# A spectrum in one matmul stage: five row blocks of weighted sines in place of sixteen blocks and a butterfly

## The chip, the cores and the metric

The kernel runs on one core of one Trainium2 chip. The metric is the device time of one execution in microseconds (us). Engines: PE (TensorE; its weight loads are counted apart, as PEld), DVE (VectorE), ACT (ScalarE), POOL (GpSimd) and SP (SyncE, which here only issues DMA transfers). Each engine works through its own instructions in their order; it waits for others by semaphores.

## The reference, cut to what matters

Two independent parts are computed, and their outputs stand side by side. Part A is a recurrent attention over 64 segments of 32 rows, which the change does not touch. Part B is a state-space layer: for each of 1024 channels d, a kernel of 2048 values is made from 128 complex exponentials, and the input u is convolved with it by transforms of twice the length.

```python
P = jnp.exp(logdA[:, :, None] * l[None, None, :])
K = jnp.einsum('dn,dnl,dn->dl', Cc, P, dB).real
Kf = jnp.fft.rfft2(Kp...)            # K, padded to 4096
Uf = jnp.fft.rfft2(up...)            # u, padded to 4096
y = jnp.fft.irfft2(Uf * Kf, ...)[..., :L] + u * Dskip
```

## The kernel before, in words

Part B runs first (0 to 670 us), part A after it (to the end at 2019.6 us). All of part B is in `part_b`; its order is written out by hand.

*Few different values.* The kernel's values are worked out at 641 of the 2048 places only: every place up to 256, every second one to 512, every fourth to 1024, every eighth to 2048 (row 640 is the last). In between, the nearest lower or upper one stands. These 641 rows are `Kd` in device memory.

*Parameters and matrices* (up to about 100 us). Sines and cosines of 16 row blocks by 4 frequency groups are made into `MF`. The transform of 4096 values is split by residue r of the place modulo 4, so that `MF` serves the kernel, the input u and (transposed, as `MI`) the way back.

*Table rounds* (about 100 to 390 us). The loop `for f in range(-1, 17)` (L1191) runs through the words of `ORDER` (L661); a word with a prime belongs to the round before. Round f makes the values of 64 channels: PE makes exponents and phases (`X..p`, `X..t`), ACT takes eight exponentials E (L1139), loads another table, and takes sine and cosine (`S`, `C`); DVE makes `wn` (L1165, word `w`), the absolute value (`b`), and the products gi and gr (L1113, L1114); PE sums the products (`K`), DVE copies the sums (`x`) into a tile `KxT`, one for each half of the channels, two buffers. The words P, U and M in between are side work: projections of part A (`P`), spectra of the input u (`U`, for the 16 blocks below, to `Ud` in device memory) and transposes of `MF` (`M`, L940, copied at L944 and written to `MId` by POOL at L945). When a half is complete, `put_values` writes its rows from `KxT` to `Kd` in 44 pieces (L1020). Those of the first half go out one at each exponential of the rounds after; those of the second half ("late writes") after round 16, from the queues of SP (24) and POOL (20) in turn.

*Loading the kernel's values.* `load_k` (L1024) fetches them back, repeated as the 2048 places need them: 32 to 64 small transfers into 16 blocks of 128 rows, `KT`. `negate` makes a negated copy of 8 of the blocks.

*Blocks.* Then come 16 blocks b: four quarters of 256 channels (dq) by four frequency groups (kc). For each,
- `spectrum` (L1091): 64 matmuls of 128x128 by 128x256 (L1101) into two PSUM tiles `hps`, one for the even and one for the odd residues;
- `odd` (L1259, three copies on ACT) and `pointwise` (L1264, DVE): sum and difference of the two tiles (`X`, L1265 and 1266), which are two frequencies n_ = 0, 1 apart by half the range; four multiplications with the spectrum of u (`us`, loaded by `load_u`), two sums, and two more to `Bt`;
- from b = 4 on, two `inverse` (L1324 and on) of an earlier quarter: 32 matmuls back each (`products_back`), a copy by ACT (L1339), a multiplication and a sum by DVE (L1342, 1343), and a transfer out.

Spectrum b+1 stands ahead of pointwise b and of the two inverses in PE's order. Blocks 0 to 3 have no inverses. Pool `ps_h` has 2 buffers up to block 3 and 3 buffers of one tile after, `ps_y` has 2. After block 15 eight inverses are left. The SBUF tiles x, y and osb of `pointwise` are in the pool `b_pw`, which takes space that the pools of the table rounds (`b_tab`, `b_kx` with `KxT`, `b_tmp`) gave back; a tile that overlaps one of them waits for whoever still reads it.

*Weights of part A.* `residents` loads 39 tiles of part A's weights into space that part B gives back; a dictionary in the block loop says how many at each block.

Of the kernel before, what the change touches and what calls it, by code (L numbers as in the profile page):

```python
# [662 lines left out]
def part_b(ctx, tc, u, A_re, A_im, B_re, B_im, C_re, C_im, log_dt, Dskip, out_b, ahead, copies, residents, first_state):  # L663
# [32 lines left out]

    par_t = [tabs.tile([128, 8, 128], BF16, name="pt%d" % n_) for n_ in range(2)]
# [337 lines left out]

    def load_k(d0, n_d, qs, KT, later=None):
        dsl = slice(d0, d0 + n_d)

        def rows(r0, n, step=1):
            return Kd[r0:r0 + step * (n - 1) + 1:step, dsl]  # L1040
        n_q = [0]

        def get(out, in_):
            q = qs[n_q[0] % len(qs)]
            n_q[0] += 1
            if later is None:
                q.dma_start(out=out, in_=in_)
            else:
                later.append(lambda: q.dma_start(out=out, in_=in_))
        for r in (0, 2, 1, 3):  # L1050
            k0 = KT[:, 4 * r, :]
            get(k0[0:64], rows(r, 64, 4))
            get(k0[64:128], rows(256 + (0, 0, 1, 2)[r], 64, 2))
            k1 = KT[:, 4 * r + 1, :]
            if r == 2:
                get(k1[0:128:2], rows(384, 64, 2))
                get(k1[1:128:2], rows(386, 64, 2))
            else:
                get(k1[:], rows(384 + (0, 0, 0, 1)[r], 128))
            for mc in (2, 3):  # L1060
                k2 = KT[:, 4 * r + mc, :]
                q0 = 512 + 64 * (mc - 2)
                get(k2[0:128:2], rows(q0, 64))
                if r == 0:
                    get(k2[1:128:4], rows(q0, 32, 2))
                    get(k2[3:128:4], rows(q0 + 2, 32, 2))
                else:
                    get(k2[1:128:2], rows(q0 + 1, 64))
        return KT
# [9 lines left out]
    KNs = []  # L1079

    def negate(KT, eng=None):
        KN = ahead.pool.tile([128, 8, DH], BF16, name="KN", tag="xTl")
        if eng:
            eng.tensor_scalar(out=KN[:], in0=KT[:, 8:16, :], scalar1=-1.0, scalar2=None, op0=ALU.mult)
        else:
            for i in range(2):
                sc.activation(out=KN[:, :, DQ * i:DQ * i + DQ], in_=KT[i][:, 8:16, :], func=ACT.Copy, scale=-1.0)
        KNs.append(KN)

    def spectrum(b, s_):  # L1090
        dq, kc = b // 4, b % 4  # L1091
        KN = KNs[dq // 2]
        d = slice(DQ * (dq % 2), DQ * (dq % 2) + DQ)
        KT = ks[0][:, :, d] if dq < 2 else ks[dq - 1][:]
        for half in range(2):
            for r in range(2):
                for cs in range(2):
                    for i, rr in enumerate((r, r + 2)):
                        for mc in range(4):
                            rhs = KN[:, 4 * (rr - 2) + mc, d] if half == 1 and i == 1 else KT[:, 4 * rr + mc, :]  # L1100
                            pe.matmul(s_[r][half][:, cs, :], lhsT=MF[:, kc, 4 * rr + mc, cs, :], rhs=rhs,  # L1101
                                      start=(i == 0 and mc == 0), stop=(i == 1 and mc == 3), skip_group_check=True)
# [94 lines left out]
    for eng, names in ((sc.copy, ON_ACT), (v.tensor_copy, ON_DVE)):  # L1197
        for nm, kind, slot in names:
            evict_of[nm] = (kind, slot, eng)
    for f in range(-1, 17):  # L1200
        if f == 15:
            for kind, slot in sorted(k for k in pending if k[0] == "P"):
                run_evict(kind, slot, v.tensor_copy)
            while ahead.late:
                ahead.late.pop(0)()
            ks = [load_k(0, DH, (sy, gp), ahead.pool.tile([128, 16, DH], BF16, name="KT", tag="kst"))]
        if f == 16:
            spectra = [load_u(0), load_u(1)]
        for word in ORDER:
            nm, r = word.rstrip("'"), f - word.endswith("'")  # L1210
            if f == 16 and word == ORDER[0]:
                s0 = ps_e.tile([128, 2, 512], F32, name="pa", tag="pa")
                s1 = [ps_t.tile([128, 512], F32, name="ptt", tag="ptt") for _ in range(2)]
                first = [[s0[:, half, :].rearrange("p (c d) -> p c d", c=2) for half in range(2)],
                         [t_[:].rearrange("p (c d) -> p c d", c=2) for t_ in s1]]
                negate(ks[0], v)
                spectrum(0, first)
            if nm in evict_of:
                run_evict(*evict_of[nm])
            elif nm[0] in side_ops:  # L1220
                if f >= 0 and r >= 0:
                    run_side(nm[0], int(nm[1:] or 0))
            elif nm[0] == "X":
                e = int(nm[1])
                if 0 <= r <= 15 - (e == 0) or (r == -1 and e == 0):
                    table_ops[nm[2]](r, e)
            elif 0 <= r <= 15:
                table_ops[nm[:-1]](r, int(nm[-1]))
    for n_, f_ in enumerate(late):
        f_((sy, gp)[n_ % 2])  # L1230
# [20 lines left out]
    KT2 = [pool.tile([128, 16, DQ], BF16, name="KT", tag="KT%d" % i) for i in range(2)]  # L1251
    MI = [pool.tile([128, 2, 2, 4, 128], BF16, name="MI", tag="MI%d" % i) for i in range(8)]
    resident = residents(pool, [MF[:, kc].rearrange("p c a n -> p (c a n)")[:, 2048 * i:2048 * i + 2048] for kc in range(4) for i in range(2)])

    def odd(s_):
        o_ = pw.tile([128, 2, 2, DQ], F32, name="osb_", tag="o")
        sc.copy(out=o_[:, 0], in_=s_[1][0])
        sc.activation(out=o_[:, 1, 0], in_=s_[1][1][:, 1, :], func=ACT.Copy, scale=-1.0)
        sc.copy(out=o_[:, 1, 1], in_=s_[1][1][:, 0, :])  # L1259
        return o_  # L1260

    def pointwise(b, s_, o_):
        kc, Bt, us = b % 4, Bs[b // 4], spectra.pop(0)
        X = pw.tile([128, 2, 2, 2, DQ], F32, name="x", tag="x")  # L1264
        v.tensor_tensor(out=X[:, 0], in0=s_, in1=o_[:], op=ALU.add)  # L1265
        v.tensor_tensor(out=X[:, 1], in0=s_, in1=o_[:], op=ALU.subtract)  # L1266
        Y = pw.tile([128, 2, 2, 2, DQ], F32, name="y", tag="y")
        for n_ in range(2):
            uc, un = (us[n_][:, :, i, :].unsqueeze(2).to_broadcast([128, 2, 2, DQ]) for i in range(2))
            v.tensor_tensor(out=Y[:, n_], in0=uc, in1=X[:, n_], op=ALU.mult)  # L1270
            v.tensor_tensor(out=X[:, n_], in0=un, in1=X[:, n_], op=ALU.mult)
        Yc, Xc = (t_[:].rearrange("p a b c d -> p (a b) c d") for t_ in (Y, X))
        v.tensor_tensor(out=Yc[:, :, 0, :], in0=Yc[:, :, 0, :], in1=Xc[:, :, 1, :], op=ALU.subtract)
        v.tensor_tensor(out=Yc[:, :, 1, :], in0=Yc[:, :, 1, :], in1=Xc[:, :, 0, :], op=ALU.add)
        for j, op in ((0, ALU.add), (1, ALU.subtract)):
            v.tensor_tensor(out=Bt[:, kc, j], in0=Y[:, 0], in1=Y[:, 1], op=op)

# [36 lines left out]
    def products_back(yp, dq, c, neg, mn, kcs):  # L1314
        r, Bt = c // 4, Bs[dq]
        j = r % 2
        for b in range(2):
            for kc in kcs:
                for cs in range(2):
# [26 lines left out]
    keys = []  # L1346
# [3 lines left out]
    ctx_h = ExitStack()  # L1350
    ps_h = ctx_h.enter_context(tc.tile_pool(name="b_psh0", bufs=2, space=PSUM))

    def halves(t_):
        return [t_[:, half] for half in range(2)]
    now = s0[:].rearrange("p h (c d) -> p h c d", c=2), odd(first)
    for b in range(16):
        dq = b // 4
        if b % 4 == 0:
            Bs[dq] = (bp0, bp)[dq % 2].tile([128, 4, 2, 2, 2, DQ], BF16, name="Bt", tag="B")
        if b == 0:  # L1360
            ks += [load_k(DQ * i, DQ, (sy, gp), KT2[i - 2], keys) for i in (2, 3)]
        if b == 3:
            nxt = [load_inverse(*todo[n_]) for n_ in range(NIV)]
            pointwise(b, *now)
            ctx_h.close()
            ctx_p.close()
            ps_h = ctx.enter_context(tc.tile_pool(name="b_psh", bufs=3, space=PSUM))
            ps_y = ctx.enter_context(tc.tile_pool(name="b_psy", bufs=2, space=PSUM))
        if b + 1 < 16:
            s_ = [ps_h.tile([128, 2, 2, DQ], F32, name="hps", tag="h") for _ in range(2)]  # L1370
            spectrum(b + 1, [halves(t_) for t_ in s_])
            then = s_[0][:], odd([halves(t_) for t_ in s_])
        if b != 3:
            pointwise(b, *now)
        now = then
        if b + 2 < 16:
            spectra.append(load_u(b + 2))
        for _ in range(min(16, len(keys)) if b >= 2 else 0):
            keys.pop(0)()
# [3 lines left out]
        for _ in range({1: 1, 2: 1, 3: 1, 6: 4, 11: 2, 12: 2, 13: 4, 14: 4}.get(b, 0)):  # L1383
# [8 lines left out]
        if b == 6:  # L1392
            negate(ks[1:])
# [4 lines left out]
    for n_ in range(8):  # L1398
        inverses(1)
        for _ in range((11, 5)[n_] if n_ < 2 else 1):  # L1400
            next(resident, None)
    while unsent:
        unsent.pop(0)()

# [27 lines left out]
def kernel(  # L1432
# [34 lines left out]
    def residents(stay, early):  # L1467
# [5 lines left out]
        four = ahead.pool.tile([128, 4, 2048], BF16, name="W4", tag="kst")  # L1473
        for t_ in [four[:, i, :] for i in range(4)]:
            put(t_)
            yield
        for n in range(2):
            for t_ in early[0:6] if n == 0 else early[6:8]:
                put(t_)
                yield  # L1480
            two = stay.tile([128, 2, 2048], BF16, name="W2", tag="KT%d" % n)
            for i in range(2):
                put(two[:, i, :])
                yield
# [77 lines left out]
```

## Time and profile before

| what | value |
|---|---|
| three runs, us | 2025.39, 2012.65, 2023.66 (median 2023.66) |
| profiled execution: time, span, us | 2021.33, 2019.6 |
| mean granted TensorE clock | 0.986 |
| busy over the span: PE, DVE, ACT, POOL | 91%, 71%, 47%, 22% |
| part B ends, last product back (L1324) | 669.7 us |
| rounds f = 0 to 15: one from the next | 20.05 us |
| block 0's first DVE sum | 429.87 us |
| block 4's first product back | 484.8 us |
| from one block to the next, 4 to 14 | 14.0 us |

The profile is of one execution; times inside it count from its start. The views quoted below have these forms. By stage: start:end, length, then the busy time of PE, PEld, DVE, ACT and POOL with the number of instructions, the granted clock (1.00 is full), DMA share and GB/s. Timelines: start, length, engine, line of the kernel, operation, output<-input, shape, and in brackets the idle time before it and who ended it; instructions of one kind that follow each other closely are one row (x64). An engine's name with q is its DMA queue.

### The profile page before, as it was taken

Reading aid. Unit: us, or ns where it says so; the run is one execution under the profiler, and the core shown is the slowest. Engines: PE = TensorE matmul, PEld = TensorE weight load, DVE = VectorE, ACT = ScalarE, POOL = GpSimd, SP = SyncE. Lnnn points to the kernel's source line nnn. Section 1 sums busy time; section 2 is a strip of 40 time slices with the busy share of each in tenths; the row PEclk is TensorE's granted clock in tenths of the full one; section 3 lists DMA queues with packets and bytes.
Section 4 is the critical chain, followed back from the end, with each engine's and each line's share of the span. In section 5 each row is a group of like instructions: output and inputs, shape, how many; then the busy total and the mean of one; then the engine's idle time right before and its main releaser. Section 6 shows DMA issues by size and latency. Waiting matters only on the chain.

```text
span 2019.6 us, 75101 instructions
## 1 busy us (share of the span) xinstructions
PE 1835.2 (91%) x32170; PEld 1154.4 (57%) x32198; DVE 1437.1 (71%) x3442; ACT 949.2 (47%) x1662; POOL 440.1 (22%) x864
## 2 busy tenths in 40 slices
PE   1699999778999789999999999999999999999998
PEld 1365766567888445555555555555555555555554
DVE  8879999999998356766667666666766666676650
ACT  4888898831333334344444434344444434344430
POOL 2135555547000011111111111111111111111120
PEclk9999999998999889999999999999999999999999
DMA  6788996868456999999999999999999999999991
GB/s 172 187 231 270 265 269 179 221 188 264 153 158 231 343 326 348 339 336 345 345 345 350 332 335 353 344 335 344 351 324 343 346 344 352 336 349 332 345 346 40
DMA packets 352630, 591.60 MB, mean 293 GB/s; under 512 B 111312, under 2 KB 229408, under 8 KB 350248
## 3 DMA queue, kind: packets, MB, share of 16 engines
q1 hardware_dynamic: 297452, 527.25, 77.2%
q10 hardware_dynamic: 44812, 28.26, 4.6%
q0 software_dynamic: 10032, 31.28, 4.4%
q8 instruction: 252, 4.13, 0.8%
q14 instruction: 82, 0.67, 0.1%
HBM read 531.12 MB, written 66.05 MB: 296 GB/s over the span
## 4 chain that ended last, share of the span: by engine, by line
PE 37%; DMA 23%; DVE 4%; issue 1%; ACT 1%; POOL 0%; SPq 0%; ACTq 0%; DVEq 0%; POOLq 0%
PE acc L375 21%; DMA wst<-WD_v 9%; PE pp L488 8%; DMA wst<-WD_o 7%; PE pe L625 3%; DMA wst<-WD_k 2%; PE tr L386 2%; DMA wst<-WD_q 2%; DMA arena<-PKd 2%; PE pv L460 1%; PE pv L456 1%; DVE arena L582 1%; PE sc L400 1%; DVE arena L441 1%; ACT arena L582 1%
## 5 line engine op out<-in xcount | busy, mean ns | idle before, releaser
L375 PEld LDWEIGHTS <-a_hT 128*32 128x32 bf16 x12352 | 326.4, 96 | 320.0 <-issue 60.9
L381 ACT CAST arena<-acc 128x512 bf16<-128x512 f32 x384 | 224.7, 585 | 396.2 <-PE acc L375 320.8
L375 PE MATMUL acc<-W,a_hT 128*32 128x512 bf16 x4608 | 354.1, 381 | 0.0
L488 PEld LDWEIGHTS <-arena 128*32 128x32 bf16 x8256 | 217.2, 97 | 86.8 <-issue 63.4
L375 PE MATMUL acc<-wst,a_hT 128*32 128x512 bf16 x2304 | 229.6, 382 | 29.3 <-DMA wst<-WD_v 22.0
L389 POOL COPY arena<-arena 128x128 bf16<-128x128 bf16 x128 | 37.4, 292 | 840.7 <-DMA arena<-PKd 315.6
L296 DVE TENSOR_SCALAR arena<-keep 128x256 int32<-128x256 int32 (+1 forms) x512 | 175.4, 394 | 29.5 <-PE acc L375 28.3
L375 PE MATMUL acc<-MF,a_hT 128*32 128x512 bf16 x2048 | 172.0, 382 | 0.0
L488 PE MATMUL pp<-W_o,arena 128*32 128x256 bf16 x4096 | 138.2, 275 | 5.0 <-DMA W_o<-in_A_Wo_dram 5.0
L168 PE MATMUL pro<-xTl,wsl 128*128 128x512 bf16 x490 | 113.0, 383 | 12.5 <-ACT xTl L112 6.6
L415 DVE TENSOR_REDUCE a_mx<-sc 128x4 f32<-128x160 f32 (+1 forms) x192 | 71.6, 373 | 73.6 <-PE sc L403 71.8
L419 ACT ACTIVATE sc<-sc 128x160 f32<-128x160 f32 (+1 forms) x192 | 63.9, 333 | 122.6 <-DVE sc L416 121.9
L1101 PEld LDWEIGHTS <-MF 128*128 128x128 bf16 x1024 | 102.5, 100 | 30.8 <-issue 8.2
L503 DVE COPY arena<-tr 128x512 bf16<-128x512 bf16 x64 | 27.2, 425 | 126.7 <-PE tr L386 126.7
L423 DVE TENSOR_REDUCE a_mx<-sc 128x4 f32<-128x160 f32 (+1 forms) x192 | 72.8, 379 | 55.3 <-ACT sc L419 54.9
L1101 PE MATMUL hps<-KT,MF 128*128 128x256 bf16 x720 | 94.2, 283 | 15.0 <-DVE x L1266 11.1
L1139 ACT ACTIVATE E<-pa 128x648 bf16<-128x648 f32 x128 | 90.9, 710 | 33.1 <-PE pa L1131 27.9
L1324 PE MATMUL yp<-Bt,MI 128*128 128x256 bf16 x680 | 102.8, 273 | 0.7 <-ACT yb L1339 0.7
L450 POOL TENSOR_TENSOR arena<-arena,a_BD 128x128 bf16<-128x128 bf16 x128 | 51.1, 399 | 234.0 <-DVE arena L433 221.5
L582 ACT CAST arena<-pp 128x128 bf16<-128x128 f32 x64 | 17.0, 265 | 163.2 <-DVE arena L582 163.2
L168 PEld LDWEIGHTS <-wsl 128*128 128x128 bf16 x512 | 50.5, 99 | 72.0 <-issue 16.2
L375 PE MATMUL acc<-W_v,a_hT 128*32 128x512 bf16 x1280 | 91.1, 378 | 0.0
(330 smaller groups left out, 3892.1 us busy)
## 6 DMA issues: line engine op xcount, KB each, us to landing
wst<-WD_v SPq DMA_DIRECT2D x256, 512.0 KB
wst<-WD_k SPq DMA_DIRECT2D x192, 512.0 KB
wst<-WD_o SPq DMA_DIRECT2D x192, 512.0 KB
wst<-WD_q SPq DMA_DIRECT2D x128, 512.0 KB
Ud<-ux POOLq DMA_DIRECT2D x16, 1024.0 KB, 5.9
uq<-Ud SPq DMA_DIRECT2D x32, 512.0 KB
wsl<-in_A_Wk_dram SPq DMA_DIRECT2D x16, 512.0 KB
wsl<-in_A_Wv_dram SPq DMA_DIRECT2D x16, 512.0 KB
```

What stands on the lines that cost most here:

```text
L168: nc.tensor.matmul(a[:], lhsT=w[:, kc, 128 * j:128 * j + 128], rhs=xTl[:, kc, :, :].rearrange("p s k -> p (s k)"), start=(kc == 0), stop=( ...
L296: nc.vector.tensor_scalar(out=out.bitcast(I32), in0=in_.bitcast(I32), scalar1=0, scalar2=None, op0=ALU.bitwise_or)
L375: nc.tensor.matmul(a[32 * g:32 * g + 32, o_:o_ + rhs.shape[1]], lhsT=hT[:, kc, :], rhs=rhs, start=(kc == 0), stop=(kc == KC - 1), tile_pos ...
L381: nc.scalar.copy(out=q, in_=a[:])
L415: nc.vector.tensor_reduce(out=m_, in_=x, axis=AX.X, op=ALU.max)
L419: nc.scalar.activation(out=flat(sc, i), in_=flat(sc, i), func=ACT.Exp, scale=scale)
L423: nc.vector.tensor_reduce(out=m_, in_=x, axis=AX.X, op=ALU.add)
L488: nc.tensor.matmul(po[32 * qt:32 * qt + 32, o_:o_ + rhs.shape[1]], lhsT=oT[:, h % 4, (h % 16) // 4, :], rhs=rhs, start=False, stop=(h == 3 ...
L625: nc.tensor.matmul(pe[n][:], lhsT=left[2 * b + hi // 16][:, 128 * (hi % 16):128 * (hi % 16) + 128], rhs=wo[u][:, 1024 * hh + 512 * n:1024 ...
L1101: pe.matmul(s_[r][half][:, cs, :], lhsT=MF[:, kc, 4 * rr + mc, cs, :], rhs=rhs, start=(i == 0 and mc == 0), stop=(i == 1 and mc == 3), ski ...
L1139: sc.activation(out=T["E", r, e // 4][:, lo:lo + 8 * NE].rearrange("p (i c) -> p i c", i=2), in_=T.pop(("p", r, e))[:, :, 0:4 * NE], func= ...
L1324: pe.matmul(yp[:, b, :], lhsT=m_[:, b, cs, kc, :], rhs=Bt[:, kc, j, half, c_, :], start=(kc == 0 and cs == 0 and half == 0), stop=(kc == 3 ...
```

## The change

The spectrum is made from the 640 different values themselves, in five blocks of 128 rows: row 0 to 255 in two, then one for each coarser range. A value that stands for several places is one sine times a weight that depends on the frequency alone; the places of a coarse row are put at the middle of its range, and the weights make up for it.
- **Matrices G.** For each group kc, n_, row block j, cosine or sine and half there is a 128x128 matrix. `columns_of_turns` makes the rows' and frequencies' digits (22 small operations on DVE, 25 on POOL) when round f = 3 begins, ahead of all of its words; `turned_columns` transposes them in the P slots of round 15. `build` then multiplies them (matmuls of 7 rows into a PSUM bank: angles in turns), and ACT takes the sine of each bank (`sine_of`, 11 of 512 columns for a group; 3 more copies for the weights). `weighted` multiplies three of the row blocks by their weights on DVE, twice a group.
- **Spectrum.** 40 matmuls for a block: five row blocks, for each n_, half, and cosine or sine. Each n_ has its own PSUM tile; nothing is summed or negated afterwards. `odd`, `negate` and the two sums `X` go. The multiplications read PSUM. All of Kd's 640 rows of a half come by one transfer.
- **Row 640** enters on the way back: one matmul of four rows for every second inverse (`l4`, `w4`, made from `Kd[640]` and rows of u by POOL).
- **Order.** At f = 16 a list of its own, `LAST`, is run, with the matrices of group 0 and the spectrum of block 0; U2 and U3 move from round 16 to 15; the last transposes' copy (`M0`) goes from DVE to ACT. The load of u for block 1 stands behind the second `weighted` of group 0. Groups 1 to 3 are built during blocks 0 to 2.
- **Weights of part A.** 39 loads as before, into other tiles; by block 14, 19 as before, at other blocks.

The core of the diff:

```diff
+    g_l = tabs.tile([128, 14, 7], BF16, name="g_l")
+    g_r = tabs.tile([128, 4, 4, 7], BF16, name="g_r")
...
+    def load_k(half, KT):
+        sy.dma_start(out=KT, in_=Kd[0:640, DH * half:DH * half + DH].rearrange("(j p) d -> p j d", p=128))
+        return KT
+
+    def columns_of_turns():
+        at = tabs.tile([128, 6], I32, name="g_at")
+        for j, (b0, step) in enumerate(((0, 2), (256, 2), (512, 4), (1024, 8), (2048, 16), (0, 2))):
+            gp.iota(at[:, j:j + 1], pattern=[[1, 1]], base=b0, channel_multiplier=step)
+        atF = tabs.tile([128, 6], F32, name="g_atF")
+        v.tensor_copy(out=atF[:], in_=at[:])
...
+    def sine_of(out, bank):
+        sc.activation(out=out, in_=bank.bitcast(I16)[:, 0:1024:2], func=ACT.Sin, scale=float(TWO_PI / 65536))
...
+    def weighted(kc, n_, amp):
+        a_ = amp.rearrange("p (j q) -> p j q", j=3)[:, :, 256 * n_:256 * n_ + 256]
+        g_ = G[kc][:, n_, 2:5].rearrange("p j s h f -> p j s (h f)")
+        v.tensor_tensor(out=g_, in0=g_, in1=a_.unsqueeze(2).to_broadcast([128, 3, 2, 256]), op=ALU.mult)
...
-    def spectrum(b, s_):
...
-                    for i, rr in enumerate((r, r + 2)):
-                        for mc in range(4):
-                            rhs = KN[:, 4 * (rr - 2) + mc, d] if half == 1 and i == 1 else KT[:, 4 * rr + mc, :]
-                            pe.matmul(s_[r][half][:, cs, :], lhsT=MF[:, kc, 4 * rr + mc, cs, :], rhs=rhs,
+    def spectrum(b, n_, outs):
...
+            for cs in range(2):
+                for j in range(5):
+                    pe.matmul(outs[half][:, cs, :], lhsT=G[kc][:, n_, j, cs, half, :], rhs=KT[:, j, d], ...)
...
+    LAST = ("w0' b0' C0' b1' gi0' C1' G0 gr0' w1' gr1' gi1' K0' K1' G1 x0' x1' G2 M0 G3 m0").split()
     for f in range(-1, 17):
+        if f == 3:
+            columns_of_turns()
...
-        X = pw.tile([128, 2, 2, 2, DQ], F32, name="x", tag="x")
-        v.tensor_tensor(out=X[:, 0], in0=s_, in1=o_[:], op=ALU.add)
-        v.tensor_tensor(out=X[:, 1], in0=s_, in1=o_[:], op=ALU.subtract)
+        Y, Z = (pw.tile([128, 2, 2, 2, DQ], F32, name=nm, tag=nm) for nm in "yz")
         for n_ in range(2):
...
+                    v.tensor_tensor(out=t_[:, n_, h], in0=us[n_][:, h, i, :].unsqueeze(2).to_broadcast([128, n_h, 2, DQ]), in1=x_, op=ALU.mult)
...
+                if kc == 3 and b == 1 and c % 4 == 2:
+                    pe.matmul(yp[:, b, :], lhsT=l4[:, r, :], rhs=w4[:, DQ * dq:DQ * dq + DQ], ...)
...
+        points = pointwise(b, now)
+        next(points)
...
+        if b < 3:
+            for n_ in range(2):
+                weighted(b + 1, n_, amp)
+        if b < 2:
+            make(b + 2, 6)
...
-            s_ = [ps_h.tile([128, 2, 2, DQ], F32, name="hps", tag="h") for _ in range(2)]
-            spectrum(b + 1, [halves(t_) for t_ in s_])
-            then = s_[0][:], odd([halves(t_) for t_ in s_])
-        if b != 3:
-            pointwise(b, *now)
+            now = []
+            for n_ in range(2):
+                now.append([ps_h.tile([128, 2, 2, DQ], F32, name="hps", tag="h")[:]])
+                spectrum(b + 1, n_, [now[n_][0][:, half] for half in range(2)])
+        next(points)
...
-        for _ in range({1: 1, 2: 1, 3: 1, 6: 4, 11: 2, 12: 2, 13: 4, 14: 4}.get(b, 0)):
+        for _ in range({1: 2, 2: 2, 3: 1, 7: 2, 11: 4, 12: 2, 13: 3, 14: 3}.get(b, 0)):
             next(resident)
```

In the changed kernel the multiplications of a block (four on DVE, to tiles y and z of `b_pw`) stand ahead of the next spectrum, and the sums behind it.

More of the change, by code (lines that the diff above doesn't have):

```diff
@@ new lines, in part_b, with turned_columns, evict @@
+    G = {}
+    def turned_columns():
+        for i in range(4):
+            pt = take([128, 8, 128], BF16, "gt")
+            for c in range(8 if i != 1 else 6):
+                pe.transpose(out=pt[0:7, c, :], in_=g_l[:, 8 * i + c, :] if i < 2 else g_r[:, 2 * (i - 2) + c // 4, c % 4, :], identity=ident[:])
+            def evict(copy, i=i, pt=pt):
+                flat = pt[0:7].rearrange("p c n -> p (c n)")
+                if i == 0:
+                    copy(out=G["lhs"][:, 0:1024], in_=flat)
+                elif i == 1:
+                    copy(out=G["lhs"][:, 1024:1408], in_=flat[:, 0:384])
+                    copy(out=G["wts"], in_=flat[:, 384:768])
+                else:
+                    copy(out=G["rhs"][:, 1024 * (i - 2):1024 * (i - 2) + 1024], in_=flat)
+            yield evict
@@ L1207, in part_b @@
+            side_ops["P"] = (turned_columns(),)
         if f == 16:
-            spectra = [load_u(0), load_u(1)]
-        for word in ORDER:
+            amp0 = ahead.pool.tile([128, 2048], BF16, name="amp", tag="wsl", bufs=4)[:, 0:1536]
+            spectra = [load_u(0)]
+            made = build(0, lambda: take([128, 512], F32, "gf"), amp0)
+        for word in ORDER if f < 16 else LAST:
             nm, r = word.rstrip("'"), f - word.endswith("'")
[L1211 to L1218, printed above, removed]
+            if f == 16 and nm[0] in "GMm" and not word.endswith("'"):
+                if nm == "G0":
+                    for _ in range(9):
+                        next(made)
+                elif nm == "G1":
+                    weighted(0, 0, amp0)
+                elif nm == "G2":
+                    for _ in made:
+                        pass
+                    s0 = ps_e.tile([128, 2, 512], F32, name="pa", tag="pa")
+                    s1 = [ps_t.tile([128, 512], F32, name="ptt", tag="ptt") for _ in range(2)]
+                    now = [[s0[:].rearrange("p h (c d) -> p h c d", c=2)], [t_[:].rearrange("p (h c d) -> p h c d", h=1, c=2) for t_ in s1]]
+                    spectrum(0, 0, [now[0][0][:, half] for half in range(2)])
+                elif nm == "G3":
+                    weighted(0, 1, amp0)
+                    spectrum(0, 1, [t_[:, 0] for t_ in now[1]])
+                    spectra.append(load_u(1))
+                elif nm == "M0":
+                    run_side("M", 0)
+                else:
+                    run_evict("M", 0, sc.copy)
+            elif f == 15 and nm == "P4":
+                run_side("U", 2)
+            elif f == 15 and nm == "p4":
+                run_evict("U", 2, sc.copy)
+            elif nm in evict_of:
@@ L1255, in odd @@
[L1255 to L1262, printed above, removed]
+    gF = ahead.pool.tile([128, 16384], BF16, name="gF", tag="MF")
+    G.update({kc: part_of(gF, 5120 * (kc - 1)) for kc in (1, 2, 3)})
+    resident = residents(pool, [gF[:, 2048 * i:2048 * i + 2048] for i in range(8)])
@@ L1349, in part_b, with make @@
     Bs = [None] * 4
[L1350 to L1355, printed above, removed]
+    ctx_h, ctx_f = ExitStack(), ExitStack()
+    ps_f = ctx_f.enter_context(tc.tile_pool(name="b_psf", bufs=4, space=PSUM, side="right"))
+    l4 = k1[0:4, 2560:3072].rearrange("p (r n) -> p r n", r=4)
+    w4 = k1[0:4, 3072:4096]
+    makes = [build(kc, lambda: ps_f.tile([128, 512], F32, name="gf", tag="f"), amp) for kc in (1, 2, 3)]
+    def make(kc, n):
+        for _ in range(n):
+            next(makes[kc - 1])
+    make(1, 14)
     for b in range(16):
@@ L1369, in part_b @@
         if b + 1 < 16:
-            s_ = [ps_h.tile([128, 2, 2, DQ], F32, name="hps", tag="h") for _ in range(2)]
-            spectrum(b + 1, [halves(t_) for t_ in s_])
-            then = s_[0][:], odd([halves(t_) for t_ in s_])
-        if b != 3:
-            pointwise(b, *now)
-        now = then
+            now = []
[3 more added lines that the diff above has]
+        next(points)
+        if b < 2:
+            make(b + 2, 8)
         if b + 2 < 16:
             spectra.append(load_u(b + 2))
-        for _ in range(min(16, len(keys)) if b >= 2 else 0):
-            keys.pop(0)()
         if b < 4:
@@ L1472, in residents, with some @@
             yield
-        four = ahead.pool.tile([128, 4, 2048], BF16, name="W4", tag="kst")
-        for t_ in [four[:, i, :] for i in range(4)]:
+        def some(where, tag, n):
+            t_ = where.tile([128, n, 2048], BF16, name="W%d" % n, tag=tag)
+            return [t_[:, i, :] for i in range(n)]
+        for t_ in some(stay, "KT1", 2):
             put(t_)
             yield
[L1477 to L1484, printed above, removed]
-        two = ahead.pool.tile([128, 2, 2048], BF16, name="W2", tag="xTl")
-        for i in range(2):
-            put(two[:, i, :])
+        for t_ in some(ahead.pool, "xTl", 2):
+            put(t_)
+            yield
+        for t_ in some(ahead.pool, "kst", 4) + early:
+            put(t_)
             yield
@@ L1504, in residents @@
             put(places.pop(0)())
+            yield
+        for t_ in some(stay, "KT0", 2):
+            put(t_)
             yield
```

174 lines of the change are left out of this document (113 added, 61 removed).

## The prediction

> **What bounds the kernel now.** First the busy time by stage (start:end, length, then busy us of each engine, granted clock, DMA share, GB/s), then the timelines of the engines and queues at the places that the change touches (start, length, engine, line, what; in brackets the idle time before it and who ended it).
>
> ```profile
> 100.00:390.00 290.00, 284.05 (x3565) 190.16 (x3584) 262.22 (x409) 257.02 (x291) 135.31 (x162) 1.00 0.86 238
> 390.00:430.00 40.00, 25.65 (x489) 19.35 (x487) 34.47 (x53) 27.13 (x27) 22.92 (x32) 0.82 0.77 225
> 430.00:478.00 48.00, 34.34 (x258) 27.52 (x257) 47.16 (x40) 3.41 (x9) 28.12 (x50) 0.87 0.78 244
> 478.00:640.00 162.00, 161.26 (x1483) 144.19 (x1481) 151.47 (x161) 53.39 (x80) 26.59 (x55) 1.00 0.55 175
> 640.00:670.00 30.00, 28.22 (x260) 24.72 (x261) 13.06 (x24) 12.29 (x14) 0.00 (x0) 1.00 0.92 314
> 670.00:735.00 65.00, 45.63 (x747) 22.40 (x750) 27.00 (x78) 17.41 (x35) 5.56 (x14) 0.79 0.92 333
> ```
>
> Rounds of tables fill 100 to 390; blocks 0 to 3 lie in 430:478, where DVE (the third sum) is busy 47.16 of 48; blocks 4 to 14 lie in 478:640, where PE is busy 161.26 of 162. Part A follows at 670. What a change gives in blocks 4 to 14 is therefore set by PE, until something else is longer.
>
> ```profile
> 540.67 7.15 PE L1324 MATMUL yp<-Bt,MI 128*128 128x256 bf16 x64
> 547.66 4.09 PE L1101 MATMUL hps<-KT,MF 128*128 128x256 bf16 x36
> ```
>
> 64 products back start in 6.99 us, 0.109 us each; a block has 64 of them and 64 of the spectrum: 14.0 us. DVE needs 11.84 us for the pointwise part and 1.4 for two outputs, so it almost keeps pace:
>
> ```profile
> 548.55 0.42 DVE L1343 TENSOR_TENSOR uu<-uu,yb 128x512 bf16<-128x512 bf16 x1 [0.16 <-ACT yb L1339]
> 548.89 1.22 DVE L1265 TENSOR_TENSOR x<-hps,osb__8231 128x1024 f32<-128x1024 f32 x1
> ...
> 562.87 1.22 DVE L1265 TENSOR_TENSOR x<-hps,osb__8399 128x1024 f32<-128x1024 f32 x1
> ```
>
> In the rounds the bound is a ring: ACT's table load waits for DVE's last product, and DVE's first instruction waits for ACT's sine. A round takes 20.05 us.
>
> ```profile
> 156.19 0.37 DVE L1165 TENSOR_SCALAR wn<-sn 128x768 bf16<-128x768 bf16 x1 [0.24 <-ACT sn L1152]
> ```
> ```profile
> 162.06 1.28 ACT L1139 ACT_TABLE_LOAD   x1 [0.40 <-DVE gr L1114]
> ```
> ```profile
> 156.41 1.30 POOL L945 DMA_DIRECT2D MId<-ms  x1 [1.77 <-DVE ms L944]
> ```
>
> Last, the writes of the kernel's values after the last round, on two queues, and how long one takes from issue to landing:
>
> ```profile
> 429.25 16.06 SPq L1020 DMA_DIRECT2D Kd<-KxT  x24
> ```
> ```profile
> 439.72 0.64 POOL L1020 DMA_DIRECT2D Kd<-KxT  x1 [4.17 <-issue]
> ...
> 457.71 0.52 POOL L1020 DMA_DIRECT2D Kd<-KxT  x1 [0.49 <-DMA Kd<-KxT]
> ```
> ```profile
> DMA to landing us min/median/max: 2.2/4.8/7.2
> ```
>
> Nobody on the path waits for them today: DVE began block 0 at 429.87, before the first landed.
>
> **The change, part by part.** The sum is made against the profiled run, 2021.33 us (span 2019.6); the median of the three runs shown is 2023.66, 2.3 above it.
>
> *Constants in round 3.* 22 small DVE instructions stand ahead of that round's `wn` on DVE, and they alternate with 25 of POOL, which stand behind the MId issue that ends at 157.7. DVE comes free at 155.9. Six iotas at 0.095 (eleven take 1.05) bring it to 158.3; the copy, then five selects of about 0.2, and the next copy: 159.9; seven conversions and copies of 0.15 to 0.2 with waits for their own results: 161; seven on partition numbers: 161.5; POOL's selects, memsets and iotas: 162.8; the last seven: 163.5. So `wn` starts 7 us late, and as it is in the ring, E of the round and everything behind is 7 us late. Ends: 3 (DVE's own 22 x 0.15, POOL hidden) and 10 (selects like L212, 1.07 us, take part). I take +7.
>
> *End of the rounds.* Two spectra-of-u steps move from round 16 into 15: 8 matmuls and one ACT copy now stand before the last E, +1.4 there. Removed from DVE are the negation (1.21) and two sums (1.2). The steps of the new matrices for group 0 (14 on ACT, 0.48 apart as copies of 512 are) follow the cosines. By these, DVE would be ready for block 0 at about 434 instead of 429.87.
>
> *The new wait.* In the built program the first multiplication of block 0 waits for the KxT writes on both queues: tile y (57152 to 65344 in a partition) now begins inside the upper KxT buffer (44800 to 57344), as the new tables moved that up by 896 bytes; before, it ended at 56448, below the first tile at 57152. SP's 24 writes start behind a load that waits for the second weighting, at 433.5, and take 16.1: 449.6. POOL's 20 stand behind the last MId write, issued at about 436 because its copy is now on ACT behind the sines; 18.0 us as now, less up to 4.4 for the gap at 448 when the block loads saturated DMA: the last issues at 452 to 458 and lands 3 to 5 later. I take 457; ends 449 (SP alone) and 462. What is queued on DVE behind it: all of block 0, and with it the loads of u for block 2 (SP), which wait for its buffers.
>
> *Blocks 0 to 3.* Per block DVE loses two sums from PSUM (2.27) and gains two weightings (1536 bf16; by 1824 in 1.03 and 768 in 0.49, 0.9 each): multiplications 4.9, weightings 1.8, sums 4.67: 11.4; without weightings 9.6. From 457, block 4 starts at 457 + 3 x 11.4 + 9.6 = 500.8, before at 479.2. ACT's 14 steps per group take 7 us of its idle time (3.41 busy of 48) and the matmuls fit beside. PE is cold here, but a spectrum half of 20 takes 4.0 then (456.36 in the PE timeline) and has 5.6. The products back of block 4 start when the spectrum of block 5 is done: 500.8 + 2.45 + 2.2 = 505.4, before at 484.8: **+20.6** (ends +13, +26).
>
> *Blocks 4 to 14.* PE loses 24 matmuls, gains one of four rows: 105 x 0.109 = 11.5. But the two halves of a spectrum now stay in PSUM until multiplied; with three buffers, the second half of the next one waits for two multiplications of this one, and these stand on DVE behind the last output of the block before. From the rows above: PE starts the next spectrum at 547.66, DVE is free at 548.89, 1.23 later; two multiplications, 2.45; so the second half starts 3.7 after the first, not 2.2. Period 3.7 + 2.2 + 7.1 = 13.0, with semaphores 13.1. Ten periods to block 14: **-9**. Ends: -25 (PE alone) and -6 (the 1.5 us that DVE lost at 535.20).
>
> *After them.* PE waited 0.69 and 1.10 at 649 and 652 for ACT behind DVE's last block; this is shorter now: -1 (0 to -1.8). The odd half's three copies on ACT were off the path: 0. The 39 loads of part A's weights stand at the same blocks, 19 by block 14; k's second load is one DMA for 32 pieces, and DMA is busy 0.55 there: 0. In 670:735 part A waits for these loads, which start from buffers that come free with the end: it moves along.
>
> Sum: 2021.33 + 7 + 20.6 - 9 - 1 = **2039 us**.
>
> A page gives another landing: the Trainium skill, DMA: Bandwidth & Descriptors (Anatomy of one DMA, SWDGE path), puts the fixed cost of a small DMA at about 2.0 us. Here the median is 4.8; by the page the sum would be some 2 us less. The measurement decides.
>
> **Rivals.**
> A. *No slower:* the writes have landed before block 0 is ready. Then block 1's weighting waits for ACT instead and block 4's products start 3.4 late: 2021.3 + 7 + 3.4 - 9 - 1 = 2021.7. It decides from a first multiplication before 439.5. Against it: SP alone needs 24 x 0.67 us from 433.5. 6%.
> B. *PE alone sets blocks 4 to 14*, 11.5 us: 2039 - 16 = 2023, no change. For it: DVE has time (11 of 13.1). Against: the third buffer. 14%.
> C. *The clock falls in every block*, because PE now pauses 1.5 us in each: both halves at 4.0 instead of 2.2, 3.3 a block, 2072. Gaps of 3.04 (444.52) left the clock full, the one of 3.25 (456.36) did not. The Trainium skill, TensorE: Matmul & The Clock Gate (A second HAM failure mode), tells of a kernel whose short pauses between PSUM banks made the clock swing; by that rule C would come. The rows here speak against it. 5%.
> D. *Round 3's delay is taken up* by pauses of later rounds: 2032. ACT has 0.4 to 0.6 us pauses per E; but the ring is closed in each round. 14%.
> E. *The writes are slower*, as before with all gaps: the start at 462, 2044. 20%.
> F. That the matmuls go and time does not follow is the forecast itself: three quarters of what PE saves is lost to waits.
>
> **How the numbers follow.** The forecast has 41%. Range 2022 to 2050: it takes in B, D, E and the upper ends of constants (+3) and blocks (+3), leaving out A, C and tails, under 2 in 10. About 1% (20 us) is what can be told from no change. Slower by over 1% of 2023.66 (2043.9) are C, most of E and a third of the forecast: 0.36. Faster by over 1% (2003) needs A and B at once: 0.04. Within: 0.60.
>
> **What would show it.** Constants: `wn` of round 3 idle for POOL for about 7 us. Wait: DVE idle some 23 us before the first multiplication of block 0, ended by a Kd write, and PE cold there. Blocks 0 to 3: starts 11.4 apart. Blocks 4 to 14: periods of 13.1, PE idle 1.5 before each second half, ended by DVE's multiplication; periods of 11.5 mean B. Wrong would be: no idle DVE at block 0, or spectra that never wait.

## The result and the profile after

The changed kernel takes 2046.11 us (median of 4 runs, 2042.74 to 2047.62), the kernel before 2023.76 (median of 4, 2012.65 to 2025.39). The ratio is 1.012, with a 95% interval of 1.0081 to 1.0159: slower by 1.2%. The forecast was 2039, range 2022 to 2050. The profiled execution took 2047.62 us, span 2045.9 (before: 2021.33 and 2019.6). So 26.3 us have to be found.

The surest way is to take the same landmarks in both traces and watch how late each is; f is the pass of the loop over rounds in which `wn` is issued.

| landmark | before | after | later by |
|---|---|---|---|
| first `wn` (f = 1) | 116.29 | 118.18 | 1.9 |
| first `wn` of f = 4 | 176.14 | 184.69 | 8.6 |
| first `wn` of f = 16 | 417.93 | 426.99 | 9.1 |
| block 0's first DVE instruction | 429.87 | 466.94 | 37.1 |
| block 4's first product back | 484.8 | 517.34 | 32.5 |
| spectrum of block 15 starts | 618.82 | 643.51 | 24.7 |
| last products back, start of the row | 669.62 | 696.34 | 26.7 |
| span | 2019.6 | 2045.9 | 26.3 |

The first 1.9 us lie ahead of everything that the change touches: other runs of the same code up to there have `wn` at 116.1 to 118.2. Then three steps show: +6.7 at f = 3, a jump at block 0, and a slow gain of 8 us over the blocks, of which 2 are lost again at the end. From f = 4 to f = 15 a round takes 19.95 us in both traces (the 20.05 of the table and of the prediction is a little high), so there nothing is won or lost.

The DVE timeline of the changed kernel at f = 3 shows the first step. DVE waits for POOL three times, 3.6 us together, ahead of `wn`, which came at 156.19 before; the small operations themselves fill the other 2.4 us between the copy's end at 157.85 and `wn`:

```profile
157.17 0.68 DVE L946 COPY ms<-mt 128x1024 bf16<-128x1024 bf16 x1
159.46 0.17 DVE L1048 CAST g_atF<-g_at 128x6 f32<-128x6 int32 x1 [1.61 <-POOL g_at L1046]
160.58 0.17 DVE L1056 CAST g_at<-g_atF 128x6 int32<-128x6 f32 x1 [0.95 <-POOL g_atF L1051]
...
163.21 0.18 DVE L1089 CAST g_kqF<-g_kq 128x32 f32<-128x32 int32 x1 [1.05 <-POOL g_kq L1087]
...
163.81 0.36 DVE L1234 TENSOR_SCALAR wn<-sn 128x768 bf16<-128x768 bf16 x1
```

The second step is one wait, again on DVE: the matrices of group 0 are weighted by 445.3, then nothing runs for 21.6 us, and what ends it is a write from KxT to device memory. The first line is block 0's first instruction in the kernel before, which waits for nothing; the others are from the changed kernel.

```profile
429.87 1.22 DVE L1265 TENSOR_TENSOR x<-pa,osb__6935 128x1024 f32<-128x1024 f32 x1
```
```profile
444.38 0.96 DVE L1151 TENSOR_TENSOR g<-g,amp 128x1536 bf16<-128x1536 bf16 x1 [2.55 <-ACT g L1120]
466.94 1.22 DVE L1366 TENSOR_TENSOR z<-uq,pa 128x1024 f32<-128x1024 f32 x1 [21.60 <-DMA Kd<-KxT]
```

The two queues that issue these writes: SP is done at 457.1, POOL at 465.4, 1.6 us before DVE goes on.

```profile
412.41 33.28 SPq L1160 DMA_DIRECT2D uq<-Ud  x4
445.74 11.38 SPq L1022 DMA_DIRECT2D Kd<-KxT  x24
```
```profile
450.16 0.56 POOL L947 DMA_DIRECT2D MId<-ms  x1 [12.43 <-ACT ms L946]
450.92 0.65 POOL L1022 DMA_DIRECT2D Kd<-KxT  x1 [0.20 <-issue]
...
461.02 4.36 POOL L1022 DMA_DIRECT2D Kd<-KxT  x8 [1.28 <-issue]
```

The stages (same columns as in the prediction): in the wait of 446 to 467 DVE is busy 0.06 of 21 us, and the granted clock falls to 0.66; from 524 to 644 it is full, but PE is busy only 108 of 120.

```profile
446.00:467.00 21.00, 13.14 (x72) 7.52 (x71) 0.06 (x1) 10.65 (x21) 11.60 (x21) 0.66 0.30 81
467.00:524.00 57.00, 43.61 (x298) 31.52 (x297) 52.70 (x51) 12.35 (x24) 17.30 (x48) 0.80 0.72 244
524.00:644.00 120.00, 108.28 (x964) 91.99 (x964) 96.97 (x109) 28.62 (x33) 0.74 (x3) 1.00 0.52 162
```

Where PE pauses there is seen in its timeline: between the halves of each spectrum, 1.22 or 1.23 us, ended by DVE's second multiplication; spectra start 13.07 us apart (13.97 before, without such a pause).

```profile
524.64 2.35 PE L1171 MATMUL hps<-k,gF 128*128 128x256 bf16 x20
528.22 2.36 PE L1171 MATMUL hps<-k,gF 128*128 128x256 bf16 x20 [1.23 <-DVE y L1366]
537.71 2.35 PE L1171 MATMUL hps<-k,gF 128*128 128x256 bf16 x20
541.28 2.36 PE L1171 MATMUL hps<-k,gF 128*128 128x256 bf16 x20 [1.22 <-DVE y L1366]
```

### The profile page after: what moved, and what is told of

Read it like the earlier page. It is cut to its first block, busy times and chain, and to the rows that moved or that the text cites. A ratio compares the mean times of both kernels' runs of the same rounds, so it can differ in the third digit from the quotient of the medians.

```text
span 2045.9 us, 74541 instructions
## 1 busy us (share of the span) xinstructions
PE 1834.5 (90%) x31928; PEld 1130.4 (55%) x31956; DVE 1411.2 (69%) x3442; ACT 958.1 (47%) x1672; POOL 415.3 (20%) x851
## 4 chain that ended last, share of the span: by engine, by line
PE 35%; DMA 24%; DVE 4%; issue 1%; ACT 1%; POOL 0%; SPq 0%; POOLq 0%; DVEq 0%; ACTq 0%
PE acc L375 18%; DMA wst<-WD_v 11%; PE pp L488 9%; DMA wst<-WD_o 5%; DMA arena<-PKd 3%; PE pe L625 3%; PE tr L386 2%; DMA wst<-WD_q 2%; DMA wst<-WD_k 2%; PE pv L456 1%; PE pv L460 1%; DVE arena L582 1%; ACT arena L582 1%; PE sc L400 1%; PE tro L588 1%
## 5 line engine op out<-in xcount | busy, mean ns | idle before, releaser
L375 PE MATMUL acc<-W,a_hT 128*32 128x512 bf16 x4608 | 334.7, 380 | 2.2 <-issue 1.2
L375 PE MATMUL acc<-gF,a_hT 128*32 128x512 bf16 x2048 | 145.6, 382 | 0.0
L1216 DVE TENSOR_SCALAR nr<-ptt 128x456 f32<-128x456 int16 x128 | 77.3, 624 | 17.7 <-PE ptt L1194 16.0
L386 PEld LDWEIGHTS <-arena 128*128 128x128 bf16 x1024 | 57.8, 98 | 54.5 <-issue 44.9
```

Of the source, the lines that this page charges most:

```text
L375: nc.tensor.matmul(a[32 * g:32 * g + 32, o_:o_ + rhs.shape[1]], lhsT=hT[:, kc, :], rhs=rhs, start=(kc == 0), stop=(kc == KC - 1), tile_pos ...
L386: nc.tensor.transpose(out=p[:, hl, :, :].rearrange("p a b -> p (a b)"), in_=q[:, 128 * hl:128 * hl + 128], identity=ident[:])
L1216: v.tensor_scalar(out=T["n", r, e // 4][:, lo:lo + 8 * NT], in0=T.pop(("t", r, e))[:, 0:8 * NT].bitcast(I16)[:, 0:16 * NT:2], scalar1=floa ...
```

## The experiments

The first four were timed against runs of the kernel before with a median of 2024.12, the next three against 2021.56, the last against 2024.83. The theory is that of the prediction: three waits, each with its place. The main rival is that the new order of work, not these waits, sets the time.

**The overlap taken away** (e1_gap), in the changed kernel:

```diff
+    gap = ctx2.enter_context(tc.tile_pool(name="b_gap", bufs=1)).tile([128, 128], BF16, name="gap")
     pw = ctx2.enter_context(tc.tile_pool(name="b_pw", bufs=1))
```

> The changed kernel with an unused pool of 256 bytes ahead of the pool of y and z, so that y begins behind the upper KxT buffer. Theory (block 0 waits for the 44 late writes because y overlaps KxT): the first multiplication of block 0 starts when its spectrum is there, at about 448.5 instead of 466.9, the rest moves along, and the time is 2046 - 17 = 2029 us (2026 to 2033). Rival 1 (something else, the load of u or the matrices, holds block 0 nearly as long): the first multiplication stays after 460 and the time is 2040 or more. Rival 2 (the writes, now beside blocks 0 and 1, delay the loads of u and MI for later blocks, and the gain is given back): the first multiplication at 448.5, but block 4 starts no more than 8 us sooner than 511.2, and the time is 2038 to 2046.

Measured: 2033.43 us (ratio 1.0053, 1.0028 to 1.0078), 0.4 above the range of the theory. Block 0 starts at 445.93, waiting 1.81 us for its spectrum and no longer for a write. But block 1 comes 15.7 us later, not 11.1: DVE now waits for the matrices of group 1, which ACT builds at its own pace. DVE timeline of e1_gap:

```profile
445.93 1.22 DVE L1367 TENSOR_TENSOR z<-uq,pa 128x1024 f32<-128x1024 f32 x1 [1.81 <-PE pa L1171]
...
453.34 0.96 DVE L1151 TENSOR_TENSOR gF<-gF,k 128x1536 bf16<-128x1536 bf16 x1 [2.67 <-ACT k L1142]
455.69 0.96 DVE L1151 TENSOR_TENSOR gF<-gF,k 128x1536 bf16<-128x1536 bf16 x1 [1.39 <-ACT gF L1120]
...
461.65 1.22 DVE L1367 TENSOR_TENSOR z<-uq,hps 128x1024 f32<-128x1024 f32 x1 [0.34 <-PE hps L1171]
```

Less the 1.9 us of the start, block 0 gains 19.1 us and block 4 (496.53 for 511.22) 12.8. The theory holds in its mechanism, and Rivals 1 and 2 fall; but a third of the wait covered other work that then shows.

**The overlap alone** (e2_shift), in the kernel before:

```diff
+    unused = tabs.tile([128, 448], BF16, name="unused")
+    gp.memset(unused[:, 0:1], 0.0)
     par_t = [tabs.tile([128, 8, 128], BF16, name="pt%d" % n_) for n_ in range(2)]
```

> The kernel before with 896 bytes per partition of an unused table, nothing else: KxT moves up as it does in the change, and the first tile of the blocks' pool (osb) overlaps it by 192 bytes. Theory: ACT's first copy to osb waits for the last late write, which lands at about 460 to 462, so block 0's first sum starts some 31 us later than at 429.9, and the time is 2024 + 29 = 2053 us (2047 to 2057). Rival (the wait in the changed kernel is due to its new order, not to the overlap): the time stays at 2024 within 4 us.

Measured: 2051.29 us (ratio 1.0133, 1.0091 to 1.0175). So 896 unused bytes cost some 27 us (2051.29 - 2024.12). ACT's first copy waits 30.39 us for a write, and block 0's first sum comes at 455.28 instead of 429.87: 25.4 us later, not 31, as the wait ended at 454.11 and not at 460 to 462. ACT timeline of e2_shift:

```profile
454.11 0.58 ACT L1259 COPY osb__6937<-ptt 128x512 f32<-128x512 f32 x1 [30.39 <-DMA Kd<-KxT]
```

**The constants in six pieces** (e3_steps): `columns_of_turns` becomes a generator with a `yield` ahead of each change between POOL and DVE, and passes f = 3 to 8 each run one piece.

```diff
         if f == 3:
-            columns_of_turns()
+            turn_steps = columns_of_turns()
+        if 3 <= f < 9:
+            next(turn_steps, None)
```

> The changed kernel with the constants of columns_of_turns cut at the places where DVE waits for POOL or POOL for DVE, in six pieces, one at the start of each of rounds 3 to 8. Theory (it is the waits between the two engines, in the ring of round 3, that cost 7 us): no wait of DVE ahead of wn; 22 short instructions spread over six rounds cost 0 to 2 us; the time is 2046 - 5 = 2041 us (2039 to 2044). Rival 1 (the delay of round 3 is taken up by later rounds anyway): 2046. Rival 2 (each round that DVE is later in by 0.3 us costs as much or more in the ring): the rounds end less than 3 us sooner, 2044.

Measured: 2040.73 us (ratio 1.0086, 1.0058 to 1.0113). `wn` of f = 3 waits 0.23 us for ACT, as before, and the first `wn` of f = 15 is at 397.90 instead of 404.17. DVE timeline of e3_steps:

```profile
157.20 0.68 DVE L946 COPY ms<-mt 128x1024 bf16<-128x1024 bf16 x1
158.12 0.37 DVE L1239 TENSOR_SCALAR wn<-sn 128x768 bf16<-128x768 bf16 x1 [0.23 <-ACT sn L1226]
```

That is 6.3 us sooner than in the changed kernel, so nothing later had taken them up. It is also more than the 3.6 us of waits: standing together ahead of `wn`, the small operations cost their own time too, and in six pieces they cost almost none (at f = 15 this version is 0.4 us behind the kernel before, apart from the start).

**A product back between the halves** (e4_between), in the changed kernel, blocks 4 to 14:

```diff
             for n_ in range(2):
+                if n_ == 1 and b >= 4:
+                    next(points)
+                    inverses(1)
                 now.append([ps_h.tile([128, 2, 2, DQ], F32, name="hps", tag="h")[:]])
                 spectrum(b + 1, n_, ...)
...
         if b >= 4:
-            inverses(2)
+            inverses(2 if b == 15 else 1)
```

> The changed kernel with the second half of each spectrum moved behind the first of the two inverses, and the sums of the pointwise part ahead of both inverses in DVE's order, in blocks 4 to 14. Theory (the second half waits 1.23 us for two multiplications because of three PSUM buffers): the wait goes, a block takes 11.7 us instead of 13.07, and the time is 2046 - 13 = 2033 us (2030 to 2037). Rival 1 (DVE, with 10.9 us of work and the waits for the copies by ACT, is the next bound): 12.4 to 12.9 a block, 2039 to 2044. Rival 2 (the period is set elsewhere): 13.07 and 2046.

Measured: 2030.75 us (ratio 1.0038, 1.0014 to 1.0062), 15 less than the changed kernel. Spectra start 11.67 us apart, and no pause is left. PE timeline of e4_between, the first half of a spectrum, its second half, and the first of the next:

```profile
523.42 2.35 PE L1171 MATMUL hps<-k,gF 128*128 128x256 bf16 x20
529.10 2.35 PE L1171 MATMUL hps<-k,gF 128*128 128x256 bf16 x20
535.09 2.35 PE L1171 MATMUL hps<-k,gF 128*128 128x256 bf16 x20
```

**All three** (e5_three), the edits of e1_gap, e3_steps and e4_between together:

> The changed kernel with three edits at once: the 256 unused bytes ahead of y and z, the constants in six pieces over rounds 3 to 8, and the second half of each spectrum behind the first inverse in blocks 4 to 14. By the runs of each alone (12.7, 5.4 and 15.4 us by the medians) and if they add up: 2046 - 33 = 2013 us (2008 to 2018), which is 0.5% below the kernel before (2024). Rival (the gains overlap, since blocks 0 to 3 are held by cold matmuls and the building of the matrices, and DMA by the weights of part A): 2020 to 2026, no faster than before.

Measured: 2006.94 us, ratio 0.9932 to the kernel before (0.9909 to 0.9955). The time is 1 us below the range, but the kernel before was 2.4 us faster in these runs than the 2024 of the forecast; the ratio forecast, 2013 to 2024 or 0.9946, lies in the interval. The gains add up, and this version beats both kernels.

**Without row 640** (e6_no_row): L1417 is left out.

> The changed kernel without the matmul of four rows on the way back (L1417): the part of row 640 is left out of the output, the rest is computed. My prediction counted each at 0.109 us. In the trace of the change the next matmul comes some 0.3 us after the one before the four-row one, so each of the 16 would cost 0.2 to 0.3. Theory A (0.109 each): 11 x 0.1 in the blocks and less after: no more than 2 us, 2044. Theory B (about 0.3 each, ten in blocks 4 to 14 and the rest behind them): the period of a block falls from 13.07 to 12.75, and the time to 2041 to 2042.

Measured: 2044.35 us, but its runs lie between 2033.65 and 2050.28 (ratio 1.0131, 1.0101 to 1.0162), so that the time tells the two theories apart badly. By its ratio this version is no faster than the changed kernel (1.012). The trace does tell them apart: spectra start 12.75 us apart instead of 13.07, so a matmul of four rows costs 0.32 us of PE, three times a full one. That is theory B for the period; the 2041 to 2042 us that it forecast were not measured. PE timeline of e6_no_row, the first halves of two spectra:

```profile
524.28 2.35 PE L1171 MATMUL hps<-k,gF 128*128 128x256 bf16 x20
537.03 2.35 PE L1171 MATMUL hps<-k,gF 128*128 128x256 bf16 x20
```

**Which queue ends the wait** (e7_m0): the last transposes and their copy ahead of the spectrum of block 0, the copy on DVE.

```diff
-    LAST = ("... G1 x0' x1' G2 M0 G3 m0").split()
+    LAST = ("... G1 x0' x1' M0 m0 G2 G3").split()
...
-                    run_evict("M", 0, sc.copy)
+                    run_evict("M", 0, v.tensor_copy)
```

> The changed kernel with the last transposes and their copy (M0, m0) ahead of the spectrum of block 0, and the copy on DVE instead of ACT; all else as in the change, the overlap too. Theory (the wait of block 0 ends when the queue of POOL has issued its 20 writes, which start behind the write of that copy): POOL's writes start at about 445 instead of 450.9, end at 459.5, and block 0's first multiplication starts at about 461 instead of 466.9; the time is 2046 - 6 = 2040 us (2038 to 2043). Rival (the writes of SP, or the landing of all of them, set the end): the first multiplication at 465 or later, 2045 to 2047.

Measured: 2039.03 us (ratio 1.0084, 1.0056 to 1.0112; the interval overlaps that of the changed kernel, so the trace decides). POOL's writes begin at 443.28 and end at 459.4, 6 us sooner than in the changed kernel; SP's end at 457.4, where they ended at 457.1; and block 0 starts at 461.90, 5.0 sooner (0.8 of it are the start's). So POOL's queue set the end. POOL's and DVE's timelines of e7_m0:

```profile
443.28 0.65 POOL L1022 DMA_DIRECT2D Kd<-KxT  x1
...
455.63 3.77 POOL L1022 DMA_DIRECT2D Kd<-KxT  x7 [0.94 <-issue]
```
```profile
461.90 1.22 DVE L1366 TENSOR_TENSOR z<-uq,pa 128x1024 f32<-128x1024 f32 x1 [16.34 <-DMA Kd<-KxT]
```

**POOL's last sums held back** (e8_held), in the kernel of e5_three: a copy of one element from DVE's last product makes POOL's six sums wait for it.

```diff
+                if f == 16 and nm == "gi1":
+                    gp.tensor_copy(out=g_l[0:1, 0, 0:1], in_=T["gi", 15, 1][0:1, 0:1])
+                    held.pop()()
```

> The kernel of the three edits, and POOL's last six sums (ux, for block 15) held back until DVE has made its last product of the tables. In the runs so far DVE's last products of two SBUF operands took 2.18, 1.09, 1.64 and 1.11 us beside these sums, where they take 1.12, 0.56, 1.11 and 0.57 otherwise, and the sums 5.2 us for four where they take 2.8. Theory (two engines that read SBUF at the same time hold each other up): the products take 1.1 and 0.57 again, about 3.4 us in all, the weighting that now lies beside the sums takes up to twice its 0.94 us, and block 0's first multiplication and all behind it come 2.5 to 3.5 us sooner: 2007 - 3 = 2004 us. Rival 1 (the products are slow for another reason, such as their place behind the table load or DMA): they stay at 2.18 and 1.64. Rival 2 (blocks 0 and 1 wait for ACT's sines and for cold matmuls anyway): products fast, block 4 no sooner, 2007.

Measured: 2010.82 us (ratio 0.9943, 0.9921 to 0.9965), which can't be told from e5_three (0.9932); the 2004 of the theory did not come. In the trace the products are fast again, the weighting beside the sums takes 2.14 us, and the last product back starts at 656.44 instead of 662.92, of which 2.0 are the start's. What part B gains here does not show in the time: after the last product back this execution took 1352.6 us (2009.0 - 656.44), that of e5_three 1347.8.

## Why the prediction was right, step by step

- **Constants, +7:** 6.7 (8.55 less the 1.89 of the start; 7.2 in e1_gap). The way there differs a little: `wn` of round 3 itself is 5.7 late, not 7 (POOL's MId issue ahead of it took 0.59 us, not 1.30), and the rest of the round adds 0.9. POOL has 28 small operations here, not 25. Rival D, that later rounds take it up, fell: the delay is 8.6 at f = 4 and at f = 15, and e3_steps gives it back.
- **The new wait and blocks 0 to 3, +20.6:** the row of block 4's first product is 32.5 late, less 8.6 for what came before: 23.9, inside the ends of 13 and 26. The start of block 0 was forecast at 457 and came at 458.3 on the same scale (466.94 - 8.6).

  That this is so near is partly luck. POOL's writes began at 442.3 on that scale, some 6 us later than forecast, and the wait ended 1.6 us after the last issue, not 3 to 5; the 14.5 us of the issues lie within the forecast's 13.6 to 18.0. (From 436, these give a last issue at 450 to 454; the 452 to 458 of the prediction doesn't follow from its terms.) Nor was DVE ready at 434: in e1_gap, where the wait is gone, block 0 starts at 445.93, which is some 439 without the 7.2 of the constants; in the changed kernel the wait hid these 5 us.

  Blocks 0 to 3 took 44.3 (forecast 43.8). From there to the first product 6.1, not 4.65: the spectrum of block 4 had itself waited 6.98 us for block 3's last multiplication and then took 6.4 us at a granted clock of 0.67, where that of block 5 took 4.4 at 1.00, so PE was late, not the multiplications.

  The runs e1_gap and e2_shift show the overlap as the cause from both sides. "E. The writes are slower" erred the other way: POOL's 20 issues took 14.5 us instead of 18.5, and its writes landed sooner, in a stage where DMA is busy 0.30 and not 0.78. The answer on line 1022 of the changed kernel (it covers the writes that POOL issues):

```profile
DMA to landing us min/median/max: 1.6/2.0/3.3
```

  The median is 2.0 us, not 4.8; in e1_gap, with a DMA share of 0.63 in 446 to 467, it is 3.0. The Trainium skill, DMA: Bandwidth & Descriptors (Anatomy of one DMA, SWDGE path), puts the fixed cost of one DMA at about 2.0 us; the median of the quiet stage agrees with that.
- **Blocks 4 to 14, -9:** 7.9 (134.0 us from block 4's first product to the spectrum of block 15 before, 126.2 after; nine of the ten periods lie in between, each 0.90 shorter). The period of 13.07 and the pause of 1.23 are those forecast (13.1 and 1.5), and e4_between removes both at once. Rival B, PE alone, is what e4_between then reaches: 11.67. (Of the 25 us that PE alone would have given, the forecast lost 16 to waits: under two thirds, not the three quarters of F.)
- **Rival C** did not come: with a pause in every block the clock stayed at 1.00 in 524 to 644. The Trainium skill, TensorE: Matmul & The Clock Gate (A second HAM failure mode), tells of a kernel whose short pauses made the clock swing; those of 1.23 us here did not.
- **After them, -1:** wrong, +2.0. From the spectrum of block 15 to the last row it took 52.8 us, before 50.8, although that spectrum itself is 1.2 us shorter (5.75 for 6.99). Two steps failed. The term counts none of the six matmuls of four rows in this stretch, 1.9 us at 0.32 each (in the blocks they were counted, at 0.109). And PE's waits for ACT did not shrink: they were 1.79 us before (0.69 and 1.10) and are 2.97 now (0.69 and the two below). Without row 640 (e6_no_row) the stretch takes 49.5 us and the waits 1.69; why the wait at 685.54 goes with the row is not shown. PE timeline of the changed kernel:

```profile
677.26 0.28 PE L1423 MATMUL yp<-Bt,mn 128*128 128x256 bf16 x1 [1.26 <-ACT mn L1389]
685.54 0.28 PE L1423 MATMUL yp<-Bt,mn 128*128 128x256 bf16 x1 [1.02 <-ACT mn L1389]
```

- **Part A, 0:** -0.4.

Together 1.9 + 6.7 + 23.9 - 7.9 + 2.0 - 0.4 = 26.2, against 26.3 of the spans and a forecast of 17.6. Of the 8.6 us between them, 1.9 are the start of that execution, 3.3 blocks 0 to 3, 1.1 blocks 4 to 14 and 3.0 the end, less 0.3 and 0.4 for the constants and part A.

## What to carry to other kernels

A tile that overlapped an older one waited here for the older one's last reader, and these 192 bytes of overlap cost 12.7 us in the changed kernel (e1_gap), more than the 7.9 that blocks 4 to 14 won: when a change adds tables, look at where the pools behind them come to lie. A saving on the bounding engine pays only as far as the waits beside it allow; the order of the same work (a product back between two halves) was worth 1.4 us a block. Compare landmarks inside the trace, not only times: part A, whose instructions no edit touched, took 1343 to 1355 us in the ten profiled executions, and that spread is wider than the gain of some edits.

## What the hardware showed that was not expected

DVE and POOL, both reading SBUF, held each other up. DVE's products of the last round took up to twice as long beside POOL's sums, and four of these took 5.20 us instead of 2.78 (POOL at 431.55 in the trace of after, at 411.90 in that of before). That is some 4 us on DVE in all, which in the changed kernel lie ahead of the wait and so cost nothing. DVE timeline of the changed kernel:

```profile
430.39 2.18 DVE L1182 TENSOR_TENSOR gi<-E,sn 128x1824 bf16<-128x1824 bf16 x1
432.50 1.09 DVE L1183 TENSOR_TENSOR gi<-E,wn 128x768 bf16<-128x768 bf16 x1
```

The same two instructions in e8_held, with the sums held back:

```profile
421.30 1.12 DVE L1191 TENSOR_TENSOR gi<-E,sn 128x1824 bf16<-128x1824 bf16 x1
422.34 0.57 DVE L1192 TENSOR_TENSOR gi<-E,wn 128x768 bf16<-128x768 bf16 x1
```

The Trainium skill, SBUF — State Buffer (Who interferes with whom), has this rule: a DVE instruction with two SBUF inputs contends with a POOL instruction that reads SBUF, and the ports that they share are an exclusive lock. The sums of the two engines agree with that. From 428.61 to 436.90, DVE took 8.29 us for six instructions that take 4.34 in e8_held (420.28 to 424.62); POOL's six sums took 9.24 (427.51 to 436.75) for 5.24 (417.47 to 422.71). Each is 4.0 us longer, about what the other needs alone, as it would be if they took turns. The trace books both engines as busy throughout (8.29 and 8.15 us in 428.6 to 436.9), so the turns themselves can't be seen in it. Two of these six instructions of DVE (`nr`, 1.87 us for 1.11, and `wn`, 0.88 for 0.35) have only one tile as input and slowed as well, which the rule quoted does not cover.
